# Attention tile loads and second-layer weight transfers put behind the attention matmul bursts in a planned xLSTM and two-layer MLP kernel

## The chip, the cores and the metric

The kernel runs on one core of a Trainium2 chip. The metric is the device time of one execution in microseconds (us). Engines are named as in the profile: PE is TensorE's matmul side, PEld its weight loads, DVE is VectorE, ACT is ScalarE, POOL is GpSimd, SP is SyncE, which here issues all data transfers.

## What is computed

An mLSTM attention over 4 batches, 8 heads, 768 steps and head size 40, and behind it two dense MLP layers on the 3072 x 320 result:

```python
C = f_stab * C + i_stab * (v k^T)
n = f_stab * n + i_stab * k
y = sigmoid(o) * (C q) / max(|n q|, 1)

h = x @ w_in          # 320 -> 2048
x = max(0.01 * h, h) @ w_out
h = x @ w_in2
x = (h * cos(h)) @ w_out2
```

Gates are stabilised by a running maximum, `m`. The weights come as float64 and are used in two float32r halves.

## The kernel before

**Work.** The sequence is cut into 12 chunks of 64 steps; a chunk of two batches is one attention tile, 24 in all (`ORDER`, line 90). A tile gives 128 rows of the MLP's input. The first layer takes these rows in eight blocks of 4, 2, 3, 3, 3, 3, 3 and 3 tiles (`BLOCKS1`), the second in eight blocks of 3. A block runs over 16 slices of the 2048 hidden columns; a slice is eight input matmuls (`m_in`, line 871), a nonlinearity on ScalarE and VectorE with a split into a high and a low half, and three output matmuls per tile (`m_out`, line 939). While a block of the first layer runs, the attention tiles of the next block are made between its slices. Layer 2 has no attention.

**An attention tile.** `a_qk` loads q and k (two loads), `a_fb` the forget factors (two loads of broadcast rows), `a_kvo` k, v and the output gate. VectorE scans the factors (`a_scan`), scales v and k (`a_vext`, `a_kt`) and weighs the scores (`a_weigh`). From tile 6 on (`FUSED`) one task of small TensorE matmuls, `a_fused` (line 666, matmuls at line 681), holds what tile c still needs of TensorE (its output and its state update) and what tile c+1 needs first (its scores and its part from the old state). In the text this is the burst of tile c; its key in the plan is `("out", c)`. Behind it come `a_ys`, `a_norm`, `a_scale` and `a_gate` (line 784, writes tile x), and x is transposed (`x_turn`, line 523) for the block.

**Weights.** Each of the 32 slices of weights is loaded as raw 64-bit words (`w_load`, line 429) and decoded by ScalarE and VectorE (`w_bits`, `w_tail`, `w_sign`, `w_round`, `w_mask`). Those of layer 1 stay in SBUF. Those of layer 2 are decoded during layer 1, stored to memory (`w_store`, line 458) and loaded again (`w_reload`) when the last block of layer 1 lets go of its slices.

**Order.** `Schedule.run` (line 107) is a planner that runs when the kernel is built. Every task has a due time `prio`, an engine with an estimated duration, `deps` (tasks that must be done in the plan), rings it takes and frees (buffers), and at times an earliest start `after`. The planner simulates engines and one DMA pipe; at each step it takes the task that can start first, and among those within 0.02 us the one with the smallest `prio`. The result is a fixed order of instructions for each engine. On the chip an instruction waits only for the data and buffers that it touches, in that order; `deps` makes no semaphore by itself. SP too issues its transfers in this order, each waiting for its buffer.

Due times of attention tasks are a tile's target `t_need` less an offset: `OFF` and `OFF0` for early tiles, `OFF1` (line 80) for tiles 6 and later. Loads, scan and some others of a fused tile count from the target of the tile before (`e1`, line 796). For the weights of layer 2 the due times of the decoding are spread evenly from `t0` to `t1` (line 498, from `W2`). Rings: q and k (`raw`) 3 buffers, `kvo` 3, `fb` 2, raw weights 3, decoded weights `wf` 4, output tiles `o` 2. `fb` of tile c is let go by the burst of tile c, `raw` of tile c by the burst of c-1, `kvo` of tile c by its burst and its gate.

Of the kernel before, what the change touches and what calls it, by code (L numbers as in the profile page):

```python
# [21 lines left out]
B, H, S, D = 4, 8, 768, 40  # L22
P = 128
# [4 lines left out]
NC = B * NCI  # L28
DP = 48
HD = H // 2  # L30
E1 = D + 1
# [7 lines left out]
KV = OO + DM  # L39
O_C, O_S = HD * E1, 512 - HD * E1  # L40
FUSED = 6
# [4 lines left out]
WC = 3 * P + DM  # L46
# [22 lines left out]
PACED = [10.0, 100.0]  # L69
TURNS = {0: -2.528, 1: -18.819}  # L70
GATES_TOO = -11.804
W2 = {0: -14.132, 1: -44.746}
OFF = {
    "fb": 135.274, "kvo": -62.905, "qk": 98.808, "vext": 3.999, "scan": -61.587, "kt": 2.172, "s": 10.837, "weigh": 64.711, "out": 101.947,
    "sig": 32.187, "ym": 41.146, "ys": -6.596, "norm": 54.306, "scale": -49.255, "gate": -53.487, "state": 112.532, "decay": 89.366, "tr": 0.153,
# [2 lines left out]
}  # L78

OFF1 = {  # L80
    "fb": 34.118, "kvo": -42.575, "qk": 35.553, "vext": 6.558, "scan": 27.336, "kt": -15.482, "s": -73.643, "weigh": -9.209, "out": 14.51, "sig": -4.322, "ym": 69.268, "ys": 98.299, "norm": -20.307, "scale": 155.47, "gate": 171.825, "state": 137.837, "decay": -16.852, "tr": 139.583,
}


# [101 lines left out]
def mlstm_moe(ctx, tc, qk, kvo, gates, w1, w2, out):  # L186
# [24 lines left out]
    col = cp.tile([P, NS, 3, 2 * H], F32, name="col")  # L211
# [7 lines left out]
    sch = Schedule()  # L219
# [13 lines left out]
    def dvp(n):  # L233
        return ("DVE", 0.065 + n * 0.00105)
# [10 lines left out]
    def dma(cols, parts=P, pace=False):  # L245
        return dict(size=cols * 4 * parts / 255e3, pace=pace)

    SP = ("SP", 0.45)
# [173 lines left out]
    wt, wraw, wf, wsg = {}, {}, {}, {}  # L422
# [46 lines left out]
        w = wt[l, i]  # L469
        on[eng].tensor_tensor(w[:, 1, :], wf.pop((l, i)), w[:, 0, :].bitcast(F32), ALU.subtract)  # L470

    def plan_decode(l, i, p, after=0.0):
        k = (l, i)
        wide = dma(2 * WC if double[l] else WC, pace=True)
        if not double[l]:
            sch.add(("wload", k), p - 6, SP, w_load, l, i, take=[("wf", k, 1)], after=after, **wide)
            return ("wload", k)
        sch.add(("wload", k), p - OFF["w_load"], SP, w_load, l, i, take=[("raw64", k, 1)], after=after,
                **wide)
        sch.add(("bits", k), p, ("DVE", 0.435, "port"), w_bits, l, i, deps=[("wload", k)], take=[("wf", k, 1)])  # L480
        sch.add(("tail", k), p, act(WC), w_tail, l, i, deps=[("wload", k)])
        sch.add(("sign", k), p + 0.1, act(WC), w_sign, l, i, deps=[("wload", k)], take=[("sg", k, 1)])
        sch.add(("round", k), p + OFF["w_round"], [dve(WC)] + pool(WC, l), w_round, l, i, deps=[("bits", k), ("tail", k), ("sign", k)],
                free=[("raw64", k)])
        sch.add(("mask", k), p + OFF["w_mask"], dve(WC), w_mask, l, i, deps=[("round", k), ("sign", k)], free=[("sg", k)])
        return ("mask", k)
# [6 lines left out]
    def plan_weights():  # L493
        for i in range(NF):
            p = t_slot[0, 0, i] - DEC_LEAD
            plan_split(0, i, p + OFF["w_hi"], plan_decode(0, i, p))
        n = len(BLOCKS1) - 1
        t0, t1 = t_slot[0, 2, 0] + W2[0], t_slot[0, n, 0] - W2[1]
        for i in range(NF):
            p = t0 + (t1 - t0) * i / NF  # L500
            dep = []
            if double[1]:
                d = plan_decode(1, i, p, after=p - 8)
                sch.add(("wstore", i), p + 3, SP, w_store, i, deps=[d], free=[("wf", (1, i))], **dma(WC))
                dep = [("wstore", i)]
            p = t_slot[0, n, i] + 6
            sch.add(("reload", i), p - 8, SP, w_reload, i, deps=dep, take=[("wf", (2, i), 1)], after=p - 9, **dma(WC))
            k = (1, i)
            sch.add(("whi", k), p, [act(WC), dve(WC, True)], w_hi, 1, i, deps=[("reload", i)], take=[("w", k, 1)])
            sch.add(("w", k), p + 0.1, [dve(WC)] + pool(WC), w_lo, 1, i, deps=[("whi", k)], free=[("wf", (2, i))])  # L510
# [275 lines left out]
    heads, heads_ps = ("ACT", 1.78), ("ACT", 1.45)  # L786

    def plan_attention(n, c, j, m):
# [5 lines left out]
        g, late = s // NG, n > 1  # L794
        fused, sc = c >= FUSED, ("out", c - 1) if c > FUSED else ("s", c)
        e1 = t_need[c - 1] if c > FUSED else e
        for hh in range(2):
            sch.add(("qk", c, hh), e1 - off["qk"] + 0.1 * hh, SP, a_qk, c, hh, take=[] if hh else [("raw", c, 1)],
                    deps=[("qk", c, 0)] if hh else [], **dma(10 * P, DP, pace=True))
        sch.add(("kvo", c), e1 - off["kvo"], SP, a_kvo, c, take=[("kvo", c, 2)], **dma(KV, pace=True))  # L800
        if c < SPREAD:
            sch.add(("fb", c), e - off["scan"] - 2, ("PE", 1.15), a_spread, c, deps=[("cut", 0), "ident"],
                    take=[("acc", ("fp", c), 1), ("fb", c, 1)])
        else:
            for r in range(2):
                sch.add(("fb", c, r), e1 - off["fb"] + 0.1 * r, SP, a_fb, c, r, deps=[("fb", c, 0) if r else ("sf", g)],
                        take=[] if r else [("fb", c, 1)], **dma(H * T, T))
        sch.add(("scan", c), e1 - off["scan"], ("DVE", 1.13) if c < SPREAD else ("DVE", 1.13, "port"), a_scan, c,
                deps=([("fb", c)] if c < SPREAD else [("fb", c, 0), ("fb", c, 1)]) + ["eye"],
# [2 lines left out]
        kt = []  # L812
# [9 lines left out]
            sch.add(("s", c), e - off["s"], ("PE", 0.66 + (0.45 if s else 0)), a_scores, c, deps=ready(c),  # L822
                    take=[("p", (c, a), 1 + (not own) + (not last)) for a in range(2)])
        if s:
            sch.add(("ym", c), e1 - off["ym"], ("DVE", 0.8) if fused else [dvp(H * E1), heads_ps], a_inter, c, deps=[sc, ("col", min(g, 1))], take=[("y", c, 1)],
                    free=[("p", (("s", c) if c == FUSED else c - 1, a)) for a in range(2)] if fused else [])
        sch.add(("weigh", c), e1 - off["weigh"], dvp(4 * P), a_weigh, c, deps=[sc, ("scan", c)] + kt, free=[("tr", ("s", c))] if fused else pair_)
        sch.add(("sig", c), e - off["sig"], ("ACT", 0.36), a_sig, c, deps=[("kvo", c), ("exp", 0, 0), ("exp", 0, 1)], table="sig")
# [276 lines left out]
```

## Time and profile before

| what | value |
|---|---|
| runs | 816.35, 817.06, 820.85 us; median 817.06 |
| the profiled execution's own time | 815.58 us |
| its span, first to last instruction | 813.8 us |
| PE, PEld busy | 98%, 94% |
| DVE, ACT, POOL busy | 77%, 54%, 3% |
| granted TensorE clock, mean | 0.998 of full speed |
| moved by DMA | 74.49 MB, 92 GB/s in the mean |

The profile shows one execution. Matmuls are pipelined, so a busy PE is one that always has a matmul under way, not one at its peak. Durations below are from this execution; its span is 1.8 us shorter than its time. The median of the runs is 1.5 us above it.

### The profile page before, as it was taken

To read this page: it belongs to the slowest core of one execution; us is meant where nothing else is said; L and a number is where in the kernel's file an instruction comes from. 1 tells how busy PE (TensorE), PEld (TensorE's weight loads), DVE (VectorE), ACT (ScalarE), POOL (GpSimd) and SP (SyncE) were. 2 spreads that over 40 slices of the span, in tenths; PEclk is the share of its full clock that TensorE was granted. 3 is DMA by queue.
4 is the path that set the end of the run, shared out by engine and by line. 5 is a ranking of instruction groups with operands and counts; after the bars stand their busy time and mean duration, and the time that the engine had idled before them with its cause. 6 is when DMAs were issued, how large, how long until landed. Compare 5 with 4: busy or idle time off the path is not lost.

```text
span 813.8 us, 19227 instructions
## 1 busy us (share of the span) xinstructions
PE 799.1 (98%) x7807; PEld 768.0 (94%) x7818; DVE 623.4 (77%) x1324; ACT 438.9 (54%) x961; POOL 21.6 (3%) x33
## 2 busy tenths in 40 slices
PE   8989999999999999999999999999999999999998
PEld 4669899999999999999999999999999999999998
DVE  8889968558475577655657788889797988888885
ACT  4569644434444444443445656556565656565664
POOL 1000001011000000000000000000000000000000
PEclk9999999999999999999999999999999999999999
DMA  5667535336253435413325201000000000010000
GB/s 160 213 210 232 163 102 194 103 121 177 87 168 102 164 95 176 144 60 125 124 96 185 97 9 33 17 18 29 21 25 25 25 25 26 15 35 10 17 10 24
DMA packets 29944, 74.49 MB, mean 92 GB/s; under 512 B 4384, under 2 KB 13728, under 8 KB 29856
## 3 DMA queue, kind: packets, MB, share of 16 engines
q1 hardware_dynamic: 29856, 73.27, 28.1%
q8 instruction: 61, 1.00, 0.5%
q14 instruction: 27, 0.22, 0.1%
HBM read 59.54 MB, written 13.71 MB: 90 GB/s over the span
## 4 chain that ended last, share of the span: by engine, by line
PE 86%; DVE 7%; DMA 3%; ACT 2%; issue 1%; ACTq 0%; SPq 0%; DVEq 0%
PE acc L939 37%; PE ph L871 34%; PE pair L871 6%; PE pair L681 2%; PE tr L523 2%; DMA kvo<-kvo 2%; PE busy L274 2%; DMA raw<-w 2%; PE sc L681 1%; DVE gl L919 1%; DVE fb L688 1%; ACT ph L880 1%; DVE wf L455 1%; DVE y L756 0%; DVE x L784 0%
## 5 line engine op out<-in xcount | busy, mean ns | idle before, releaser
L939 PE MATMUL acc<-w,gh 128*128 128x320 f32 x1568 | 347.4, 309 | 0.0
L871 PE MATMUL ph<-xt,w 128*128 128x384 f32 (+2 forms) x1760 | 344.7, 338 | 2.1 <-DVE gl L919 1.9
L871 PEld LDWEIGHTS ph<-xt,w 128*128 128x128 f32 x1760 | 298.0, 189 | 7.6 <-DVE gl L919 2.6
L939 PEld LDWEIGHTS acc<-w,gh 128*128 128x128 f32 x1568 | 265.6, 188 | 1.8
L939 PE MATMUL acc<-w,gl 128*128 128x320 f32 (+1 forms) x784 | 239.0, 308 | 0.4 <-DVE gl L919 0.4
L939 PEld LDWEIGHTS acc<-w,gl 128*128 128x128 f32 x784 | 146.3, 188 | 0.6 <-DVE gl L919 0.6
L919 DVE TENSOR_TENSOR gl<-ph,gh 128x384 fp32r<-128x384 f32 (+2 forms) x124 | 68.7, 554 | 89.9 <-ACT ph L880 86.4
L879 ACT ACTIVATE gh<-ph 128x384 fp32r<-128x384 f32 (+2 forms) x124 | 60.8, 490 | 124.3 <-PE ph L871 105.7
L901 ACT ACTIVATE r<-r,hpi 128x384 f32<-128x384 f32 x128 | 78.9, 616 | 69.9 <-DVE r L897 69.8
L224 ACT CAST gh<-g 128x384 fp32r<-128x384 f32 x128 | 65.6, 513 | 39.9 <-PE acc L939 17.2
L919 DVE TENSOR_TENSOR gl<-g,gh 128x384 fp32r<-128x384 f32 x127 | 70.4, 559 | 9.2 <-ACT gh L224 9.2
L907 DVE TENSOR_TENSOR g<-ph,r 128x384 f32<-128x384 f32 x96 | 52.6, 555 | 13.9 <-ACT r L901 12.7
L880 ACT ACTIVATE ph<-ph 128x384 f32<-128x384 f32 (+2 forms) x124 | 60.6, 489 | 0.0
L871 PE MATMUL pair<-xt,w 128*128 128x384 f32 x288 | 55.9, 336 | 0.0
L896 DVE SCALAR_TENSOR_TENSOR r<-t,ph 128x384 f32<-128x384 f32 x96 | 53.2, 554 | 3.3
L887 ACT ACTIVATE t<-ph 128x384 f32<-128x384 f32 x96 | 46.7, 487 | 13.6 <-PE ph L871 8.0
L893 DVE TENSOR_SCALAR t<-t 128x384 f32<-128x384 f32 x128 | 45.6, 356 | 7.0 <-ACT t L887 4.1
L897 DVE TENSOR_SCALAR r<-r 128x384 f32<-128x384 f32 x128 | 46.1, 360 | 4.4
L871 PEld LDWEIGHTS pair<-xt,w 128*128 128x128 f32 x288 | 49.4, 188 | 0.0
L224 ACT CAST xt<-tr 128x256 fp32r<-128x256 f32 x104 | 27.6, 316 | 25.2 <-PE tr L523 23.1
L470 DVE TENSOR_TENSOR w<-wf,w 128x704 fp32r<-128x704 f32 x32 | 28.3, 888 | 2.3 <-ACT w L224 1.9
L443 ACT ACTIVATE raw<-raw 128x704 f32<-128x704 uint32 x32 | 27.3, 853 | 3.6 <-DMA raw<-w 3.4
(120 smaller groups left out, 707.0 us busy)
## 6 DMA issues: line engine op xcount, KB each, us to landing
raw<-w SPq DMA_DIRECT2D x32, 704.0 KB, 4.5
kvo<-kvo SPq DMA_DIRECT2D x24, 484.0 KB, 3.6
raw<-qk SPq DMA_DIRECT2D x48, 192.0 KB, 3.7
w2d<-wf SPq DMA_DIRECT2D x16, 352.0 KB, 3.0
wf<-w2d SPq DMA_DIRECT2D x16, 352.0 KB, 3.1
fb<-sfd SPq DMA_DIRECT2D x40, 128.0 KB, 3.4
x2d<-o SPq DMA_DIRECT2D x24, 160.0 KB, 1.8
x<-x2d SPq DMA_DIRECT2D x24, 160.0 KB, 2.2
```

Source lines behind the costliest of these rows:

```text
L224: nc.scalar.copy(dst, src)
L871: nc.tensor.matmul(ph[:, :N], w[:, a:a + P], x[:, b, :N], start=k == 0, stop=k == 7)
L879: nc.scalar.activation(t["gh"][:, :N], h, AF.Prelu, alpha=0.01)
L880: nc.scalar.activation(h, h, AF.Prelu, alpha=0.01)
L887: nc.scalar.activation(t["a"][:, :N], t["h"][:, :N], AF.Copy, scale=1.0 / TWO_PI, bias=0.25)
L893: nc.vector.tensor_scalar(a, a, MAGIC, -MAGIC, ALU.add, ALU.add)
L896: nc.vector.scalar_tensor_tensor(r, a, -TWO_PI, t["h"][:, :N], ALU.mult, ALU.add)
L897: nc.vector.tensor_scalar(r, r, -4.712388, 1.5707959, ALU.max, ALU.min)
L901: nc.scalar.activation(r, r, AF.Sin, bias=hpi)
L907: nc.vector.tensor_tensor(t["g"][:, :N], t["h"][:, :N], t["r"][:, :N], ALU.mult)
L919: on[eng].tensor_tensor(t["gl"][:, :N], t["g"][:, :N], t["gh"][:, :N].bitcast(F32), ALU.subtract)
L939: nc.tensor.matmul(po, a[:, s], w[:, b, e], start=i == 0 and k == 0 and j < 3, stop=i == NF - 1 and k == 2, skip_group_check=True,)
```

## The change

Four things are edited. (1) The offsets `OFF1` of tiles 6 and later, and `W2`, get other values. (2) The loads of a tile c of 8 or more (q and k, k-v-o, forget factors) get a planner dependency, `gap`, on the burst of tile c-2. (3) The raw load of the i-th weight slice of layer 2 loses its earliest start and depends in the plan on the burst of tile 8+i (at most 22), with a due time just behind that burst's; its store depends on the burst of tile 9+i (at most 23) in the same way. (4) The planner's duration of `ym` for fused tiles goes from 0.80 to 0.92 us. No operation is added, removed or reshaped.

```diff
--- before.py
+++ after.py
@@ -69,7 +69,7 @@
 PACED = [10.0, 100.0]
 TURNS = {0: -2.528, 1: -18.819}
 GATES_TOO = -11.804
-W2 = {0: -14.132, 1: -44.746}
+W2 = {0: -5.09, 1: -46.716}
 OFF = {
     "fb": 135.274, "kvo": -62.905, "qk": 98.808, "vext": 3.999, "scan": -61.587, "kt": 2.172, "s": 10.837, "weigh": 64.711, "out": 101.947,
     "sig": 32.187, "ym": 41.146, "ys": -6.596, "norm": 54.306, "scale": -49.255, "gate": -53.487, "state": 112.532, "decay": 89.366, "tr": 0.153,
@@ -78,7 +78,7 @@
 }
 
 OFF1 = {
-    "fb": 34.118, "kvo": -42.575, "qk": 35.553, "vext": 6.558, "scan": 27.336, "kt": -15.482, "s": -73.643, "weigh": -9.209, "out": 14.51, "sig": -4.322, "ym": 69.268, "ys": 98.299, "norm": -20.307, "scale": 155.47, "gate": 171.825, "state": 137.837, "decay": -16.852, "tr": 139.583,
+    "fb": 141.244, "kvo": -44.251, "qk": 83.644, "vext": 2.87, "scan": -51.184, "kt": 39.885, "s": -10.115, "weigh": 55.797, "out": 25.103, "sig": 106.513, "ym": -18.386, "ys": 85.126, "norm": 53.109, "scale": 23.084, "gate": 57.877, "state": 152.634, "decay": -90.507, "tr": 175.728,
 }
 
 
@@ -469,13 +469,13 @@
         w = wt[l, i]
         on[eng].tensor_tensor(w[:, 1, :], wf.pop((l, i)), w[:, 0, :].bitcast(F32), ALU.subtract)
 
-    def plan_decode(l, i, p, after=0.0):
+    def plan_decode(l, i, p, after=0.0, gap=()):
         k = (l, i)
         wide = dma(2 * WC if double[l] else WC, pace=True)
         if not double[l]:
             sch.add(("wload", k), p - 6, SP, w_load, l, i, take=[("wf", k, 1)], after=after, **wide)
             return ("wload", k)
-        sch.add(("wload", k), p - OFF["w_load"], SP, w_load, l, i, take=[("raw64", k, 1)], after=after,
+        sch.add(("wload", k), gap[1] if gap else p - OFF["w_load"], SP, w_load, l, i, deps=gap[:1], take=[("raw64", k, 1)], after=after,
                 **wide)
         sch.add(("bits", k), p, ("DVE", 0.435, "port"), w_bits, l, i, deps=[("wload", k)], take=[("wf", k, 1)])
         sch.add(("tail", k), p, act(WC), w_tail, l, i, deps=[("wload", k)])
@@ -500,8 +500,10 @@
             p = t0 + (t1 - t0) * i / NF
             dep = []
             if double[1]:
-                d = plan_decode(1, i, p, after=p - 8)
-                sch.add(("wstore", i), p + 3, SP, w_store, i, deps=[d], free=[("wf", (1, i))], **dma(WC))
+                c = [min(FUSED + 2 + i + j, NC - 1) for j in range(2)]
+                q = [t_need[x] - OFF1["out"] for x in c]
+                d = plan_decode(1, i, p, gap=[("out", min(c[0], NC - 2)), q[0] + 0.2])
+                sch.add(("wstore", i), q[1] + 0.1, SP, w_store, i, deps=[d, ("out", c[1])], free=[("wf", (1, i))], **dma(WC))
                 dep = [("wstore", i)]
             p = t_slot[0, n, i] + 6
             sch.add(("reload", i), p - 8, SP, w_reload, i, deps=dep, take=[("wf", (2, i), 1)], after=p - 9, **dma(WC))
@@ -794,16 +796,17 @@
         g, late = s // NG, n > 1
         fused, sc = c >= FUSED, ("out", c - 1) if c > FUSED else ("s", c)
         e1 = t_need[c - 1] if c > FUSED else e
+        gap = [("out", c - 2)] if c - 2 >= FUSED else []
         for hh in range(2):
             sch.add(("qk", c, hh), e1 - off["qk"] + 0.1 * hh, SP, a_qk, c, hh, take=[] if hh else [("raw", c, 1)],
-                    deps=[("qk", c, 0)] if hh else [], **dma(10 * P, DP, pace=True))
-        sch.add(("kvo", c), e1 - off["kvo"], SP, a_kvo, c, take=[("kvo", c, 2)], **dma(KV, pace=True))
+                    deps=[("qk", c, 0)] if hh else gap, **dma(10 * P, DP, pace=True))
+        sch.add(("kvo", c), e1 - off["kvo"], SP, a_kvo, c, deps=gap, take=[("kvo", c, 2)], **dma(KV, pace=True))
         if c < SPREAD:
             sch.add(("fb", c), e - off["scan"] - 2, ("PE", 1.15), a_spread, c, deps=[("cut", 0), "ident"],
                     take=[("acc", ("fp", c), 1), ("fb", c, 1)])
         else:
             for r in range(2):
-                sch.add(("fb", c, r), e1 - off["fb"] + 0.1 * r, SP, a_fb, c, r, deps=[("fb", c, 0) if r else ("sf", g)],
+                sch.add(("fb", c, r), e1 - off["fb"] + 0.1 * r, SP, a_fb, c, r, deps=[("fb", c, 0)] if r else [("sf", g)] + gap,
                         take=[] if r else [("fb", c, 1)], **dma(H * T, T))
         sch.add(("scan", c), e1 - off["scan"], ("DVE", 1.13) if c < SPREAD else ("DVE", 1.13, "port"), a_scan, c,
                 deps=([("fb", c)] if c < SPREAD else [("fb", c, 0), ("fb", c, 1)]) + ["eye"],
@@ -822,7 +825,7 @@
             sch.add(("s", c), e - off["s"], ("PE", 0.66 + (0.45 if s else 0)), a_scores, c, deps=ready(c),
                     take=[("p", (c, a), 1 + (not own) + (not last)) for a in range(2)])
         if s:
-            sch.add(("ym", c), e1 - off["ym"], ("DVE", 0.8) if fused else [dvp(H * E1), heads_ps], a_inter, c, deps=[sc, ("col", min(g, 1))], take=[("y", c, 1)],
+            sch.add(("ym", c), e1 - off["ym"], ("DVE", 0.92) if fused else [dvp(H * E1), heads_ps], a_inter, c, deps=[sc, ("col", min(g, 1))], take=[("y", c, 1)],
                     free=[("p", (("s", c) if c == FUSED else c - 1, a)) for a in range(2)] if fused else [])
         sch.add(("weigh", c), e1 - off["weigh"], dvp(4 * P), a_weigh, c, deps=[sc, ("scan", c)] + kt, free=[("tr", ("s", c))] if fused else pair_)
         sch.add(("sig", c), e - off["sig"], ("ACT", 0.36), a_sig, c, deps=[("kvo", c), ("exp", 0, 0), ("exp", 0, 1)], table="sig")
```

## Rows read from the trace of the kernel before

**Rows 1.** The page: busy time (share, instructions) of TensorE; queue 8 (packets, MB, share).

```profile
PE 799.1 (98%) x7807; PEld 768.0 (94%) x7818; DVE 623.4 (77%) x1324; ACT 438.9 (54%) x961; POOL 21.6 (3%) x33
...
q8 instruction: 61, 1.00, 0.5%
```

**Rows 2.** Waits of TensorE: us in total, times, longest us.

```profile
PE pair L681 <- issue: 1.8, 1, 1.8
PE tr L523 <- DVE x L784: 1.7, 6, 0.5
```

**Rows 3.** Timeline of TensorE in the burst of tile 8: start us, us, instruction.

```profile
144.67 0.25 PE L681 MATMUL pair<-state,raw 40*64 40x41 f32 x1 [1.79 <-issue]
```

**Rows 4.** Windows: length; busy (instructions) of five engines; PEclk, DMA share, GB/s.

```profile
131.13:133.05 1.92, 1.92 (x130) 1.87 (x129) 0.90 (x2) 0.54 (x2) 0.00 (x0) 1.00 0.08 19
141.06:145.04 3.98, 2.19 (x129) 1.99 (x128) 1.28 (x3) 0.54 (x2) 0.00 (x0) 1.00 0.63 244
145.04:148.51 3.47, 3.47 (x17) 3.47 (x15) 3.18 (x8) 1.30 (x4) 0.73 (x1) 0.51 0.34 99
148.51:150.34 1.83, 1.83 (x15) 1.83 (x15) 1.03 (x4) 1.59 (x4) 0.00 (x0) 1.00 0.00 0
```

**Rows 5.** Window and DMA queue 8 from 500 to 600 us, in layer 2.

```profile
500.00:600.00 100.00, 100.00 (x635) 99.91 (x634) 86.47 (x197) 62.56 (x132) 0.00 (x0) 1.00 0.08 26
...
q8 instruction: 5, 0.08, 0.3%
```

**Rows 6.** DMA queues: all from 133.9 to 142.1 us; queue 8 from 142.1 to 143.1.

```profile
q1 hardware_dynamic: 555, 1.82, 67.6%
...
q8 instruction: 1, 0.02, 5.9%
```

**Rows 7.** Timeline of SP ahead of the burst of tile 8.

```profile
137.82 0.35 SPq L599 DMA_DIRECT2D kvo<-kvo  x1
138.21 0.43 SPq L429 DMA_DIRECT2D raw<-w  x1
```

**Rows 8.** The page's DMA issues: count, KB each, median us to landing.

```profile
raw<-w SPq DMA_DIRECT2D x32, 704.0 KB, 4.5
kvo<-kvo SPq DMA_DIRECT2D x24, 484.0 KB, 3.6
raw<-qk SPq DMA_DIRECT2D x48, 192.0 KB, 3.7
w2d<-wf SPq DMA_DIRECT2D x16, 352.0 KB, 3.0
...
fb<-sfd SPq DMA_DIRECT2D x40, 128.0 KB, 3.4
```

**Rows 9.** Windows of 5 us that end with bursts, and one full stretch.

```profile
128.00:133.00 5.00, 5.00 (x153) 4.80 (x151) 3.32 (x7) 2.30 (x8) 0.00 (x0) 1.00 0.46 143
...
164.30:169.30 5.00, 5.00 (x150) 4.81 (x148) 1.05 (x3) 1.90 (x6) 0.00 (x0) 1.00 0.24 94
...
330.30:335.30 5.00, 5.00 (x149) 4.75 (x147) 2.32 (x4) 2.57 (x6) 0.00 (x0) 1.00 0.04 15
341.30:346.30 5.00, 5.00 (x149) 4.75 (x147) 2.98 (x7) 2.28 (x6) 0.00 (x0) 1.00 0.81 265
...
140.09:141.05 0.96, 0.96 (x8) 0.77 (x6) 0.93 (x3) 0.66 (x2) 0.69 (x1) 1.00 1.05 403
```

**Rows 10.** Waits of SP's queue: us in total, times, longest us.

```profile
SPq L579 <- PE pair L681: 72.0, 16, 8.7
...
SPq L599 <- DVE x L784: 39.0, 16, 5.2
```

**Rows 11.** Groups of VectorE instructions, 100 to 404 us: busy, mean ns, idle before.

```profile
L604 DVE TENSOR_TENSOR_SCAN fb<-fb,eye 128x512 f32<-128x512 f32 x18 | 22.0, 1221 | 0.8 <-DMA fb<-sfd 0.6
...
L623 DVE TENSOR_TENSOR kvo<-kvo,fb 128x320 f32<-128x320 f32 x10 | 4.9, 486 | 0.1
```

**Rows 12.** Window from 100 to 404 us, columns as in rows 4.

```profile
100.00:404.00 304.00, 299.76 (x4035) 290.46 (x4034) 198.79 (x412) 130.15 (x332) 17.19 (x22) 0.99 0.40 129
```

## The prediction

> **What bounds the kernel now.** Read the page's head first: TensorE is busy for 799.1 us, 98% of the span, so a change off TensorE is worth what it takes out of TensorE's own row [rows 1]. Next the waits of TensorE, longest first: in the stretch that the change touches two count. One is 1.8 us in one piece before an attention matmul, with "issue" as its end (nothing that the profile shows was waited for); the other are six waits, 1.7 us together, of the transposes for the gated tile [rows 2].
>
> The 1.8 us deserve the timeline. The burst of a tile (64 fp32 products, each two matmuls and two weight loads in the trace) is normally short: the one at 131.13 us gives way to the next large matmul 1.92 us later. The next burst, at 141.06 us, runs dry before its last matmuls and goes on at 144.67 us after 1.79 us of idle time [rows 3], so that 3.98 us pass [rows 4]. Then look behind it: the same eight matmuls of line 871 and six of line 939 take 3.47 us at a granted clock of 0.51 (1.2 GHz instead of 2.4), and 1.83 us at 1.00 right afterwards [rows 4]. Before it fell, the engine had stood idle for that 1.79 us. So **one stall costs 2.06 + 1.64 = 3.70 us**.
>
> What ran out? Not operands: no semaphore ended it. What does arrive by DMA is code. The page has 61 packets of kind "instruction" on queue 8 [rows 1]; in a stretch of layer 2 five come in 100 us, in which TensorE starts 635 matmuls and 634 weight loads [rows 5], so one packet serves about 254 instructions. A burst uses 130 + 129 in under 2 us [rows 4], as much as a whole packet. In the 8.2 us up to 142.1 us queue 8 moved nothing, while the data queue was busy at 67.6%; the packet came in the next microsecond [rows 6]. What filled it was a kvo load let go by tile 7's gate (line 784) at 137.82 us and a 704 KB raw weight load right after it [rows 7], which together take long to land [rows 8]. I read the stall as a late code packet behind those loads. Of the 17 bursts from 131 us on, in windows of 5 us that end with them, five had the transfers busy at 0.46 to 0.81 and twelve at 0.24 or less; one of the five stalled, none of the twelve [rows 9]. A loaded queue is needed, but so is the place of the packet's border in the burst.
>
> **The change, part by part.** No instruction is added or removed; due times and two kinds of planner dependency move.
>
> The gap. `deps` is known to the planner alone: on the chip an SP entry waits for buffers. But SP works in order, and fb of tile c has two buffers, so its first load waits for the burst of c-2; SP does this 16 times already, 72.0 us in all [rows 10]. With fb's due time moved from 34 to 141 us ahead, it is planned first behind the burst, and qk (84 ahead), the weight load, and kvo (44 behind) stand after it. The wait thus holds on the chip for tiles from 8 on. Queued behind it on SP are also the x2d stores that free the output buffers, and for them the evacuations and TensorE's accumulators. The number of fb waits is unchanged, so I cost this at nothing. With that cover gone the bound is SP's longest fb wait, 8.7 us, if at a block's end a store stood behind it with both output buffers full.
>
> At the burst of tile 8 the kvo load of tile 10 and the weight load are no longer in flight: both now come behind it. The 3.70 us go. What is late next: the code packet that a burst asks for now meets fb and qk behind the burst, but there TensorE uses about 13 instructions per us [rows 5], not 130.
>
> Earlier bursts. Bursts are due 25.1 instead of 14.5 us before their tile's due time. The gate chain behind them may end earlier against its transposes: bounds are a gain of all 1.7 us [rows 2] and a loss of as much, if the new order drifts the other way. I take a gain of half of it, 0.9 us, since the due time is earlier; not more, because the planner still puts a transpose as soon as it thinks it ready.
>
> Later loads. Before, kvo of tile c+3 was let go by the gate of c [rows 10]; now kvo of c+2 comes last behind the burst of c. Up to it SP moves 2x128 + 2x192 + 352 + 704 + 484 = 2180 KB, 2.23 MB [rows 8]. At 403 GB/s, the rate of a full stretch [rows 9], that is 5.5 us. SP needs about 0.4 us to issue the first [rows 7], and kvo's 3.6 us to landing leave, less its 484 KB at that rate (1.2), 2.4 us that do not shrink: 8.3 us. VectorE then scales k in 0.49 us, its scan (1.22 us) having been done on fb meanwhile [rows 11]: 8.8 us. The shortest distances from a burst's end to the next burst are 8.0 us (133.05 to 141.06 us [rows 4], where no weights come yet and the same sum gives 6.2) and 9.1 us (windows that end at 335.3 and 346.3 us [rows 9], less a burst). At all others it is 10 us or more. So it fits, by 0.3 us at the tightest. Cost 0; if VectorE is late, up to a microsecond per burst (rival below).
>
> Weights of layer 2. The first raw load moves behind tile 8's burst, the last two behind tile 22's. Due times of the decoding start 9.0 us later and end 2.0 us later. Same VectorE and ScalarE work, with VectorE busy 199 of the 304 us from 100 to 404 [rows 12]: nothing. The dearer `ym` (0.92 for 0.80) changes the plan's clock alone, no operation.
>
> Sum against the profiled execution (815.58 us, span 813.8): 815.58 - 3.70 - 0.9 = 811.0. The three runs have a median of 817.06, 1.5 above it, and one lies at 820.85, which is 3.8 above the median, the price of one more stall. Taking the difference from the median: **812.4 us**.
>
> The Trainium skill speaks against the main term. "Runtime: NRT & Kernel Launch", section on instruction fetch mechanics, says the sequencer fetches the next 16 KiB block of 256 instructions while it executes, at a cost that is mostly hidden. This trace agrees on the block (61 packets, 1.00 MB) and not on the cover: by the page the stall term would be 0 and the sum 816.2.
>
> **Rivals.** *The stall moves or was never the loads'.* For it: four bursts with loaded queues did not stall [rows 9], and every due time of tiles 6 on is new, so the packet borders fall elsewhere in the bursts; tiles 6 and 7 are not gated. Against: behind the gate no burst should find the queue loaded. If one stall like this remains, 3.70 is given back: 817.06 - 0.9, near 816 to 817. In "DMA: Bandwidth & Descriptors", on queues and rings, the Trainium skill says each DMA engine turns in rounds between its queues, packet by packet; by that rule a code packet would not wait out a bulk load, and the stall would stay. The quiet queue 8 up to 142.1 us [rows 6] leans against it, without deciding.
>
> *The tiles come late (slower).* With that slack gone, the PE sequencer, in order, waits for kt of tile c+1 at each burst and the large matmuls behind it wait too. It decides where load to kt takes longer than the distance of bursts. For it: 0.3 us is little, and transposes already wait for VectorE six times [rows 2]. Against: ten us and more at the other distances, and the planner itself counts these transfers before it places a burst. A scan that isn't hidden (1.22 us [rows 11]) less the 0.3 us is 0.9 us per burst; the time passes 821.1 from (821.1 - 813.4) / 15 = 0.5 us per gated burst on. Between the two, 0.7 us: 817.06 - 3.7 + 15 x 0.7 = 823.9 us.
>
> *Nothing happens.* Were fb not first on SP, qk and kvo would start early as before: 817.
>
> **Numbers.** Forecast (stall gone, no new wait) 0.53, its own range 810 to 814; the stall moves 0.15, was never the loads' 0.10, nothing happens 0.04; late tiles 0.18. About 0.5% can be told from no change, 4.1 us: faster is below 813.0, slower above 821.1. The forecast puts 0.47 below 813.0 and 0.06 in the same band; the next three, 0.29, are all "same" and late tiles all slower. The lower end, 809.0, is the forecast with both waits of [rows 2] gone wholly (0.8 more) and 2.6 us of a second stall; the upper end, 818.5, takes in the first rival and leaves out late tiles.
>
> **What would show it.** Right: no "issue" wait at line 681 among PE's waits; all bursts from 131 us 1.9 us long; granted clock 1.00 from 100 to 404 us, where 0.99 stood [rows 12]; DMA share in the windows that end with the bursts near 0; fb, qk, weights, kvo in this order on SP behind each burst. Wrong: an idle piece of 1 to 2 us in some other burst, or many waits at line 681 for a scaled k or a weighed score.

## The result, and the profile after

The changed kernel takes 808.32 us (median of 4 runs, 807.84 to 809.38), the kernel before 817.24 in the same comparison: ratio 0.9884 [0.9853, 0.9916], so faster by my 0.5%. I had 812.4, with 809.0 as the lower end. Against the kernel before as it ran in the batches below (815.6 to 816.5) it is 7.3 to 8.2 us less instead of 8.9. The profiled execution after takes 808.76 us, its span is 807.0.

The page after, its line of busy time and its row of queue 8 (answers to [rows 1]); then the longest waits of TensorE (us in total, times, longest us; [rows 2]):

```profile
PE 796.3 (99%) x7803; PEld 766.4 (95%) x7814; DVE 610.7 (76%) x1305; ACT 439.7 (54%) x967; POOL 42.2 (5%) x53
...
q8 instruction: 61, 1.00, 0.5%
```

```profile
PE ph L874 <- DVE gl L922: 2.2, 3, 1.5
PE busy L274 <- DVE gm L298: 1.0, 1, 1.0
PE acc L942 <- DVE gl L922: 0.6, 1, 0.6
```

The 1.8 us with "issue" as their end are gone, and so are all waits of the transposes for the gated tile. (The four instructions fewer are warm-up fillers, which the planner places by its own clock.) Windows over the bursts of tiles 7 and 8, and from 100 to 404 us (columns as in [rows 4]):

```profile
132.26:134.18 1.92, 1.92 (x130) 1.87 (x129) 0.42 (x1) 0.72 (x3) 0.00 (x0) 1.00 0.04 9
143.83:145.75 1.92, 1.92 (x130) 1.87 (x129) 0.42 (x1) 0.72 (x3) 0.00 (x0) 1.00 0.00 0
...
100.00:404.00 304.00, 302.98 (x4075) 295.87 (x4074) 191.35 (x400) 135.05 (x341) 37.80 (x42) 1.00 0.44 135
```

The burst of tile 8 takes 1.92 us instead of 3.98 [rows 4], the granted clock is 1.00 where 0.99 stood [rows 12], and TensorE is busy 3.2 us more of the 304. SP behind the burst of 175.24 us goes in the order that I had read off the due times:

```profile
176.79 0.45 SPq L581 DMA_DIRECT2D fb<-sfd  x1
177.30 0.65 SPq L574 DMA_DIRECT2D raw<-qk  x1
...
179.58 0.45 SPq L429 DMA_DIRECT2D raw<-w  x1
180.13 0.46 SPq L601 DMA_DIRECT2D kvo<-kvo  x1
```

One sign that I had named did not come: the transfers are not near 0 ahead of the bursts. Of the 16 bursts of tiles 7 to 22, four have them busy at 0.31 or more in the 5 us before, tile 22's at 0.87 and tile 20's at 0.63, and none stalls:

```profile
333.81:338.81 5.00, 5.00 (x32) 4.75 (x31) 3.92 (x7) 3.38 (x7) 0.00 (x0) 1.00 0.63 191
```

Where the time went, by the first input matmul of blocks 1, 2 and 7 in the timelines, first before, then after:

```profile
115.75 0.32 PE L871 MATMUL ph<-xt,w 128*128 128x256 f32 x1
156.14 0.34 PE L871 MATMUL ph<-xt,w 128*128 128x384 f32 x1
411.85 0.34 PE L871 MATMUL ph<-xt,w 128*128 128x384 f32 x1
```

```profile
115.52 0.32 PE L874 MATMUL ph<-xt,w 128*128 128x256 f32 x1
152.52 0.34 PE L874 MATMUL ph<-xt,w 128*128 128x384 f32 x1
405.22 0.34 PE L874 MATMUL ph<-xt,w 128*128 128x384 f32 x1
```

Behind block 7's start both take the same 402 us. So of the 6.8 us between the two spans 0.2 lie up to block 1, 3.4 in block 1 (the stall's block), 3.0 in blocks 2 to 6. The other two of the nine lie between profiled execution and median (below). The 0.2 is too small a figure for the start: the execution profiled after ran a stretch of its warm-up at half clock, the one before did not. Window over it, then block 1's start in a run with the new due times and no such stretch (e3 below), 1.8 us ahead of before:

```profile
10.70:14.10 3.40, 3.40 (x9) 0.93 (x8) 3.03 (x9) 1.61 (x2) 0.00 (x0) 0.50 0.46 107
```

```profile
113.97 0.32 PE L871 MATMUL ph<-xt,w 128*128 128x256 f32 x1
```

### The profile page after: what moved, and what is told of

It is laid out like the page before. It is cut to its first block, busy times and chain, and to the rows that moved or that the text cites. A ratio compares the mean times of both kernels' runs of the same rounds, so it can differ in the third digit from the quotient of the medians.

```text
span 807.0 us, 19223 instructions
## 1 busy us (share of the span) xinstructions
PE 796.3 (99%) x7803; PEld 766.4 (95%) x7814; DVE 610.7 (76%) x1305; ACT 439.7 (54%) x967; POOL 42.2 (5%) x53
## 4 chain that ended last, share of the span: by engine, by line
PE 93%; DVE 3%; DMA 2%; issue 1%; ACT 0%; SPq 0%; DVEq 0%; ACTq 0%
PE acc L942 41%; PE ph L874 37%; PE pair L874 6%; PE pair L683 3%; PE tr L525 2%; PE busy L274 2%; DMA kvo<-kvo 1%; PE sc L683 1%; DMA fb<-sfd 1%; DVE fb L606 1%; DVE gl L922 0%; DVE gm L313 0%; PE pair L645 0%; PE acc L711 0%; DVE w L470 0%
```

## Experiments

Medians are of ten executions unless said; "before" in one batch with them was 815.6 to 816.5. The second number is the ratio to that, with its interval; an interval that takes in 1 cannot be told from no change.

**e1, the kernel before once more.** Edit: a blank line at the end.

> The kernel before, unchanged, to see what one execution of it differs from another in. Theory A (stalls behind loads come in some executions more often than once): its spans differ in steps of 3 to 4 us, and executions above 816 us show a granted clock lower than the 0.998 of the profiled one, or a second idle piece in a burst. Theory B (the 1.5 us by which the median lies above the profiled execution are spread evenly): same clock in all, same single stall at the burst of tile 8. Both: time 816 to 818, ratio 1.00.

816.30 us, 1.0003 [0.998, 1.0025]. The mean granted clock of the ten executions runs from 0.989 to 1.000, so not the same in all (theory A). In the profiled one the stall of tile 8's burst is there again (1.5 us idle), one of 0.7 at tile 16's burst as well, and near 50 us something that the first profile does not have. The start of block 0, timelines of TensorE, first the kernel before as first profiled, then e1:

```profile
41.68 0.49 PE L523 MATMUL tr<-ident,x 128*128 128x128 f32 x3
...
43.30 2.58 PE L274 MATMUL busy<-hpi 128*128 128x512 bf16 x11
45.52 2.20 PE L871 MATMUL ph<-xt,w 128*128 128x512 f32 x8
49.63 2.12 PE L871 MATMUL ph<-xt,w 128*128 128x512 f32 x8 [1.90 <-DVE gl L919]
```

```profile
41.07 0.49 PE L523 MATMUL tr<-ident,x 128*128 128x128 f32 x3
44.92 2.19 PE L871 MATMUL ph<-xt,w 128*128 128x512 f32 x8
49.02 3.31 PE L871 MATMUL ph<-xt,w 128*128 128x512 f32 x8 [1.90 <-DVE gl L919]
```

After the same 1.90 us of idle time the same eight matmuls take 2.12 us in one execution and 3.31 in the other, in a window (49.0 to 52.5 us) whose granted clock is 0.59. So one program differs by a microsecond in block 0 and by 0.9 in a second stall; this is why its runs spread and its median lies above the execution that I reckoned from.

**Which edit? e2, e3, e12.** e2 is the changed kernel with the old due times, so it has the new dependencies and the new `ym`; e3 is the kernel before with the new due times (`OFF1` and `W2`) alone; e12 the kernel before with `OFF1` alone. (Long lines are cut at `...`, here and below.)

```diff
-W2 = {0: -5.09, 1: -46.716}                                  # e2
+W2 = {0: -14.132, 1: -44.746}
-    "fb": 141.244, "kvo": -44.251, ...
+    "fb": 34.118, "kvo": -42.575, ...
-W2 = {0: -14.132, 1: -44.746}                                # e3
+W2 = {0: -5.09, 1: -46.716}
-    "fb": 34.118, "kvo": -42.575, ...                        # e3, e12
+    "fb": 141.244, "kvo": -44.251, ...
```

> The new planner dependencies (tile loads behind the burst of c-2, weight loads and stores behind bursts) with the offsets and W2 of the kernel before. If the gain comes from loads kept out of the bursts, no idle piece at a burst and 812 to 814 us, with the waits of the transposes still there; if the gain needs the new due times, the stall stays somewhere, 815 to 818.

> The new offsets and W2 without the new dependencies. If the dependencies are what removes the stall, at least one burst stalls (3.7 us each) and 812 to 817 us; if the new due times alone do it, under 810 and no stall.

> The offsets OFF1 alone, with the W2 and the planner dependencies of before. If W2 matters little: 807 to 809 us, as with both; if the decoding's later start is what clears the burst of tile 8, a stall stays and 811 to 813.

e2: 816.32, 0.9996 [0.9978, 1.0013]. e3: 807.87 (4 runs), 0.9885 [0.9845, 0.9926]. e12: 808.57 (8 runs), 0.9917 [0.988, 0.9953]. So **the offsets of the due times bring the whole gain, and the dependencies of the title none**: without them 807.9, with them 808.3. Whether `W2` adds anything cannot be told: e3 and e12 lie 0.7 us apart, and their intervals overlap. In e2 no burst stalls, but other waits come, TensorE's list:

```profile
PE ph L874 <- DVE gl L922: 2.7, 3, 1.9
PE acc L942 <- DVE gl L922: 1.7, 4, 0.7
...
PE tr L525 <- DVE x L786: 0.8, 3, 0.5
```

In e3 the queues are loaded ahead of bursts and none stalls by more than 0.25 us. Two of its windows of 5 us that end with a burst, DMA share 0.74 and 0.78, against which [rows 9] stand:

```profile
161.71:166.71 5.00, 5.00 (x34) 4.78 (x32) 3.85 (x8) 2.19 (x6) 0.00 (x0) 1.00 0.74 253
...
224.13:229.13 5.00, 5.00 (x34) 4.81 (x33) 3.40 (x7) 1.78 (x6) 0.26 (x1) 1.00 0.78 275
```

**Is it the loads? e4, e6, e9.** The kernel before with one, two and three loads behind tile 8's burst in the plan.

```diff
-a_kvo, c, take=[("kvo", c, 2)]
+a_kvo, c, deps=[("out", 8)] if c in (10, 11) else [], take=[("kvo", c, 2)]   # e6: c == 10
-w_load, l, i, take=[("raw64", k, 1)], after=after,
+w_load, l, i, take=[("raw64", k, 1)], after=after, deps=[("out", 8)] if k == (1, 1) else [],  # e4, e6, e9
```

> The kernel before with one planner dependency more: the raw load of weight slice 1 of layer 2 behind the burst of tile 8. Theory (a late code packet behind loads): the idle piece at the burst of tile 8 goes or shrinks below 1 us, 813 to 814 us (minus 3.7). Rival (the stall has nothing to do with loads): it stays at 1.8 us, with 817.

> The kernel before with both loads that ran into the burst of tile 8 (raw weights of slice 1, kvo of tile 10) behind it in the plan. Theory (loads delay the code packet): no idle piece at that burst, 812 to 814 us. Rival: still over 1 us of idle there, as with the weight load alone, 815 to 816.

> The kernel before with the raw weight load of slice 1 and the kvo loads of tiles 10 and 11 behind the burst of tile 8 (in the run with two loads the planner had put the kvo load of tile 11 in the freed place). Theory (loads delay the code packet): no idle piece over 0.5 us at that burst and no slow clock at 145 us, 3 to 3.7 us less in block 1; 812 to 813.5 us. Rival: 0.9 us of idle stays, 814 to 816.

e4: 815.55, 0.9987 [0.9962, 1.0011], idle 1.2 us. e6: 814.0, 0.9981 [0.9954, 1.0007], idle 0.9; the planner put another kvo load into the free place. None of the three times can be told from before; the profiles decide. In e9 (814.74, 0.9986 [0.9955, 1.0016]) nothing is left in flight; windows of 1 us up to the burst at 141.51, and TensorE's wait:

```profile
139.00:140.00 1.00, 1.00 (x10) 1.00 (x9) 1.00 (x2) 0.53 (x3) 0.00 (x0) 1.00 0.00 0
140.00:141.00 1.00, 1.00 (x10) 1.00 (x10) 0.95 (x4) 0.20 (x1) 0.54 (x1) 1.00 0.00 0
141.00:142.00 1.00, 1.00 (x36) 0.81 (x39) 1.00 (x3) 0.46 (x2) 0.20 (x1) 1.00 0.00 0
142.00:143.00 1.00, 1.00 (x94) 1.00 (x85) 0.35 (x2) 0.17 (x1) 0.00 (x0) 1.00 0.16 56
143.00:144.00 1.00, 0.33 (x22) 0.21 (x14) 0.00 (x0) 0.00 (x0) 0.00 (x0) 1.00 0.80 307
```

```profile
PE pair L681 <- issue: 1.5, 1, 1.5
```

Moved bytes 0 for three microseconds, and the stall stays. **My reading of the stall falls here**: the code packet is late, it came at 142.43 us, 0.9 us into the burst, but with no load ahead of it.

**What makes the packet late? e5, e13, e15, e16.** TensorE's queue has a row that I had passed over. Semaphore waits of the queue (PEldq) at line 681 in the kernel before, from 138 to 142 us (ns least, median, most; first and last start):

```profile
L681 PEldq EVENT_SEMAPHORE  x1: 1775/1775/1775, 138.6 to 138.6; - x1
```

The burst's scores share a PSUM buffer with the transposes (tag `tr`, one buffer). The queue, which runs ahead of the matmuls, stands at the burst until VectorE has emptied the transposes of tile 7 (line 536, 140.06 + 0.28 us), that is until 140.4. In all eleven bursts of tile 8 (tile 7 in e5) that stalled by 0.9 us or more, the packet started 0.9 to 2.3 us after the end of this wait: 1.75 in the kernel before, loads in flight, and 1.62 in e9, none in flight. e5 moves the border of the packets by 126 instructions (21 warm-up matmuls in four pieces each). e13 takes the wait away: tile 7's transposes go behind the burst by hand. e15 makes such a wait at tile 8's burst in e12, where there is none.

```diff
+            for j in range(4):                                  # e5, e16
+                nc.tensor.matmul(gt["busy"][:, j * P:(j + 1) * P], i.to_broadcast([P, P]), i.to_broadcast([P, P]), ...)
+        t = order.pop(at_task('x_turn', 0, 2, 7))               # e13; x_hi and x_lo likewise
+        order.insert(at_task('m_out', 0, 1, 2, 10), t)
+        t = order.pop(at_task('x_lo', 0, 2, 7))                 # e15
+        order.insert(at_task('m_lo', 0, 1, 2, 10), t)
+            for _ in range(2):                                  # e15, in x_lo of tile 7
+                nc.vector.tensor_tensor(xt[:, 2, s], tr[:, 0, :], ...)
```

> The kernel before, with 21 of the warm-up matmuls at the start cut into four pieces each: 126 TensorE instructions more, the same columns, the same plan and the same loads. Theory (a code packet of 254 instructions late behind loads): every packet border falls about half a packet earlier in the work, so the idle piece at the burst of tile 8 goes though its loads are the same, and another loaded burst may get one; 812 to 814 us if none does. Rival (the idle piece belongs to that place or to its loads alone): it stays at tile 8, 816.

> The kernel before, with the transposes of the gated tile 7 and their two splits moved by hand from ahead of the burst of tile 8 to three slices behind it; every load stays where it was, and the packet's border falls 6 matmuls and 6 weight loads (0.02 of a packet) later in the burst. Theory now (the sequencer is held): scores and transposes share one PSUM buffer, so TensorE's sequencer stands at the burst until VectorE has emptied the transposes' buffer (1.77 us, until 140.4 us in the trace of before), asks for the next code packet only then, and the packet comes 0.9 to 1.1 us into a burst that uses 260 instructions in 1.9. Without the wait the packet comes ahead of the burst or in its first tenths: no stall, burst 1.9 us, granted clock 1.0 behind it, 3 us off: 812 to 813.5. Rival, the border alone: the stall of 1.5 to 2 us stays wherever a border falls like this, 816. Rival, the loads: they are still in flight, so the stall stays as well.

> The kernel with the new offsets alone (808.6, no stall, the border in the same place: 0.74 of a packet at the start of tile 8's burst), with VectorE's split of the transposed tile 7 put behind the scaling of k and its first part done three times over (the same values), so that it ends at about 140, half a microsecond before the burst, instead of 138.6. Nothing moves on TensorE. Theory (sequencer held): the stall of before appears, 1.2 to 2 us idle in the burst of tile 8 and a stretch at half clock behind it, 3 us more: 811 to 812.5. Rival (the border alone, or the loads, which are unchanged at a DMA share of 0.75): no stall, 808.6 and at most the 0.6 us by which VectorE is later.

> The new due times without the new dependencies (807.9), with 17 of the warm-up matmuls late in the start in four pieces each: 102 instructions more, 0.40 of a packet, so that the border falls at 0.72 of a packet at the start of tile 16's burst, where the sequencer is held for 2.35 us until 0.56 us before the burst. Theory: a stall of 1.2 to 2 us in that burst, 2 to 3.5 us more (810 to 811.5) besides what the longer warm-up costs. Rival (loads, or chance): no stall there, 808 plus the warm-up's cost.

e5: 819.22, 1.0051 [1.0025, 1.0077], slower. But the stall has moved, from tile 8's burst to tile 7's, both of which have a wait of the queue ahead (1.77 and 2.37 us):

```profile
138.72:142.44 3.72, 2.19 (x130) 2.00 (x129) 0.90 (x2) 0.64 (x2) 0.00 (x0) 1.00 0.13 47
151.88:153.80 1.92, 1.92 (x130) 1.87 (x129) 1.28 (x3) 0.54 (x2) 0.00 (x0) 1.00 0.88 352
```

The burst with the transfers at 0.88 is clean, the one at 0.13 stalls. A second idle piece, 1.1 us, stands right behind tile 14's burst, where the queue had waited 1.58 us. e13: 814.54, 0.9987 [0.997, 1.0004], 1.0 to 2.5 us above what I had expected, and not to be told from before; but the stall is gone. The code packet came at 139.31 us, 3.1 us ahead of the burst. The kvo and weight loads of before were let go only behind it, at 139.74 and 140.13 us, so this run does not show a packet that has to pass loads. Waits of the queue, the burst's window, and what TensorE waits for instead:

```profile
L681 PEldq EVENT_SEMAPHORE  x2: 51/51/51, 140.0 to 140.3; - x2
```

```profile
142.40:144.30 1.90, 1.90 (x129) 1.86 (x128) 1.19 (x3) 0.57 (x2) 0.95 (x1) 1.00 1.03 426
```

```profile
PE tr L523 <- DVE xt L536: 1.0, 1, 1.0
```

Block 1 is 2.5 us shorter than before (37.92 for 40.39), the 3.5 of the stall less this 1.0.

e15: 809.59 (8 runs), 0.9928 [0.9909, 0.9948], no stall in tile 8's burst, a miss. The wait is there, 1.64 us long and over 0.7 us ahead of the burst, but the packet came during it. e16: 810.47 (4 runs), 0.9929 [0.9901, 0.9957], no stall in tile 16's burst, a miss in the same way: a wait of 2.10 us, and the packet within it. So the wait alone is not enough; the kernel before has one of 1.81 us at tile 7's burst, too, and no stall there.

Nor is a wait always needed. e16 has an idle piece behind tile 7's burst (it begins at 132.40 us), where e3, with the same order and 102 instructions fewer ahead, has none. Waits of the queue, the 4 us up to the burst with the transfers at 0.93, and the weight loads behind it:

```profile
L686 PEldq EVENT_SEMAPHORE  x2: 51/51/51, 129.9 to 132.6; - x2
```

```profile
128.40:132.40 4.00, 4.00 (x32) 3.81 (x31) 3.26 (x8) 1.48 (x6) 0.00 (x0) 1.00 0.93 287
```

```profile
134.31 0.19 PEld L876 LDWEIGHTS ph<-xt,w 128*128 128x128 f32 x1
135.39 0.19 PEld L876 LDWEIGHTS ph<-xt,w 128*128 128x128 f32 x1 [0.89 <-issue]
```

The packet came 0.37 us into that burst. The stall of tile 16's burst in e1 is alike: in the first profile of before the same burst has the same transfers ahead (0.96 to 1.07) and nearly the same wait (0.57 us, e1 0.61, over 2.3 us ahead), but its packet came 1.5 us before the burst, in e1 0.1 us into it. And e12 has 1.1 us of idle behind tile 19's burst, with a wait of 1.82 us and the transfers at 0.86.

What all of these runs allow: a burst runs dry when the code packet that it needs comes late, and whether it needs one hangs on the packet's border. A wait of the queue can make it late with no load in flight (e9), and at tile 8 taking the wait away took the stall away (e13). Loads may make it late without such a wait (e16); no run was made to test that. Where the border lies to a dozen instructions cannot be counted from the trace, and the two misses leave this half argued.

**The transposes: e7, e14, e10.** e7 makes the planner alone believe that a transpose is ready 0.8 us later (a task on an engine that does not exist); nothing on the chip is slower, transposes just stand later on TensorE. e14 adds e13's move, e10 the three loads of e9.

```diff
+        if l == 0 and c >= FUSED:
+            sch.add(("lag", c), p, ("LAG", 0.8), lambda eng: None, deps=[dep])
+        sch.add(("tr", l, c), p, ..., deps=[dep, ...] + ([("lag", c)] if l == 0 and c >= FUSED else []), ...)
```

> The kernel before, with 0.8 us added in the plan alone between a gated tile (6 and later) and its transposes. Theory (transposes planned too early cost 3 us in blocks 2 to 6, by TensorE's start times): the waits of the transposes for line 784 go, 2 to 3 us less, 813. Rival (the gain of blocks 2 to 6 comes from elsewhere): less than 1 us, 815 to 816.

> The same hand move on top of the lag of 0.8 us that the planner puts between a gate and its transposes (which alone gave 811.0, with the stall still there). Theory: both terms together, 816.2 - 4.4 - 3.3, near 808.5, are the change's whole gain, from none of its loads and none of its due times. Rival, the gain of the due times is something else besides: the time stays at 811, or the two do not add up and it is above 810.

> The run before with the planned lag of 0.8 us before the transposes as well. If stall and transposes are the whole gain of the change, 808 to 810 us, as the changed kernel; if the new due times bring something else of over 1 us, 810 to 812.

e7: 811.03, 0.9946 [0.9923, 0.9969], by the ratio 4.4 us from this alone (2.5 to 6.3), its stall still there in the profile (2.0 us). Its blocks 2 to 6 take 252.3 us, the kernel before 255.7, the change 252.7. e14: 811.56 (5 runs), 0.9947 [0.9927, 0.9966]: 3.0 less than e13, but not the 808.5 of two full terms; its rival came, something else is in the gain. e10: 812.83, 0.9962 [0.9932, 0.9992], the stall there (1.4 us). How much the transposes cost is seen better on the weight-load side. Idle time of that engine ahead of line 523 in the kernel before, by what ended it (us, times):

```profile
  issue: 3.6, 8
  DVE x L784: 2.2, 7
```

Of these 5.8 us, 5.3 lie between 100 and 404 us (14 pieces). After the change neither line is there.

**e8 and e11**, six fillers into the idle piece at 47 us, and the earlier due time of the bursts alone (`"out": 25.103`):

> The kernel before with six more filler matmuls behind the first slice of block 0, where TensorE stands idle for 1.9 us at 47 us. Theory (this idle piece drops the clock to half for 3.4 us in most executions, about 1 to 1.7 us each time, but not in the profiled one): granted clock 1.00 at 50 us in every execution, median 1 to 1.5 us lower, near 814.5. Rival (no effect on the median): 815.5 to 816.5, and clock drops there still.

> The kernel before with one number changed, the offset of the bursts' due time, 14.51 to 25.103. If an earlier due burst is what frees the transposes, their waits go and 2 to 4 us with them (812 to 814); if not, the waits stay near 1.7 us in the list and 815 to 816.

Both are misses. e8: 816.44, 1.0008 [0.9984, 1.0032]: the idle piece is 0.6 us and in the profiled execution the clock stays up there, but the planner ordered the rest anew, with eight waits of the transposes (3.0 us). e11: 818.10, 1.0025 [0.9997, 1.0054], stall and transposes' waits (1.5 us) still there, and blocks 2 to 6 take 258.1 us, 2.3 more than before. The bursts' due time alone does not do it; no other was tried alone.

**The start: e17, e18.** In the new order the first input matmuls come ahead of filler. After the change:

```profile
42.67 0.49 PE L525 MATMUL tr<-ident,x 128*128 128x128 f32 x3
...
45.21 2.19 PE L874 MATMUL ph<-xt,w 128*128 128x512 f32 x8
47.25 0.61 PE L274 MATMUL busy<-hpi 128*128 128x512 bf16 x2
49.31 2.12 PE L874 MATMUL ph<-xt,w 128*128 128x512 f32 x8 [1.45 <-DVE gl L922]
```

From the transposes to the second group it is 6.64 us, 7.95 before. e17 puts TensorE's and ScalarE's order of that by hand into the kernel before (of its three moves, TensorE's is shown), e18 adds it to e14.

```diff
+        t = order.pop(at_task("m_in", 0, 0, 4, 0))
+        order.insert(next(i for i, u in enumerate(order) if u[3].__name__ == "g_busy" and u[0] > 41.4), t)
```

> The kernel before, with only the end of its warm-up in the order that the new offsets give, by hand: the first eight input matmuls of block 0 ahead of the last six of the eleven warm-up matmuls (43.3 to 45.5 us in the trace of before), the last part of tile 3's split ahead of a weight slice's tail and sign on ScalarE, and the first nonlinearity ahead of the next such pair. Theory: this order is the third term of the gain. From tile 3's transposes to the first slice's output matmuls the profile of before takes 9.9 us and that of after 8.6, and the idle 1.9 us at 47 us, after which some executions run at half clock, are partly filled: 1.3 to 2.2 us less, 814 to 815, with the stall at tile 8's burst and the transposes' waits unchanged. Rival (the start is noise between executions): 816, no difference.

> All three hand edits on the kernel before: the start's order, tile 7's transposes behind the burst, the lag of 0.8 us ahead of the transposes; no due time, no load and no dependency of the change. Theory: 811.6 (two of them) less 1.3 to 2.2: 809.4 to 810.3, within 2 us of the change's 808.3. Rival: the start adds nothing, 811.6, and the due times have a further part of 3 us that none of the three holds.

e17: 818.02 (12 runs), 1.0026 [1.0003, 1.005]; e18: 811.9 (6 runs), 0.9946 [0.9928, 0.9964]. A miss: no gain, e17 is slower if anything. ScalarE and VectorE of e17 say why:

```profile
46.21 0.59 ACT L880 ACTIVATE ph<-ph 128x512 f32<-128x512 f32 x1
```

```profile
46.47 0.88 DVE L470 TENSOR_TENSOR w<-wf,w 128x704 fp32r<-128x704 f32 x1
47.58 0.89 DVE L451 CUSTOM_DVE_ANT_0 wf<-raw,wf 128x1408 uint16<-128x1408 uint16 x1 [0.22 <-ACT raw L443]
48.39 0.68 DVE L919 TENSOR_TENSOR gl<-ph,gh 128x512 fp32r<-128x512 f32 x1
```

The slice was ready for its split at 46.8; VectorE, whose order I had left, decoded weights until 48.4. That the new order of VectorE is what saves this microsecond or two was not tried alone. e18's rival came: 811.9 against the change's 808.3, 3.6 us that none of the three hand edits holds. Where they lie is read against e3, which like e18's profile has no stretch at half clock up to its last 2 us: e18 is 3.4 us longer, 2.5 of it up to block 1 (116.48 against 113.97), 0.4 in block 1, 0.5 in blocks 2 to 6. So what is left is mostly the start.

## Why the prediction was wrong, step by step

- **The stall goes: right in size, half right in cause.** It was priced at 3.70, and block 1 is 3.39 shorter. The late code packet stands; "behind those loads" fell with e9: no load, and a stall. "A loaded queue is needed" fell with it. The rival "never the loads'" (0.10) had that, but its time (816 to 817) assumed that the stall would then stay; the new order did away with the queue's wait at the same time. After the change no burst from 131 us on has a wait of its queue above 0.1 us. That the forecast size came out is luck in part: the gate on the loads was to bring it, and e3 has it without the gate.
- **"Earlier bursts", 0.9: the step that failed.** I took half of the 1.7 us in TensorE's list [rows 2] and called that sum the bound. It was none. Ends of matmuls are modelled and overlap the next start (in the timeline above the eleven fillers end at 43.30 + 2.58 = 45.88, the next group starts at 45.52), so a gap between groups hides in busy time; the weight-load side shows 5.8 us in 15 pieces. Measured: 3.0 us in the pair of profiles, 3.0 (medians of e13 and e14) to 4.4 (e7, by its ratio). The mechanism was wrong as well: bursts that are due earlier, alone, left the waits (e11); transposes planned later against their gates took them away (e7).
- **The start: not in the sum.** I took the new due times of tiles 6 and later to act on the bursts alone. But the order at the end of the warm-up changed too: 1.3 us less from transposes to the second group than in the first profile of before, 2.5 less to that group's end where the clock fell (e1), and 1.8 less up to block 1 where it did not (e3). Why is argued: the loads of tile 6 stand among the weight loads of the warm-up. The hand order of e17 did not bring it.
- **The baseline.** A profiled execution of before without the clock's fall near 50 us was the base, and the median carries it in part; after the change the idle piece is 1.45 instead of 1.90 us and its profile shows no fall. The nine us of the medians are thus 6.8 of the profiles and some two of executions that the old order disturbs more often. The granted clocks on record bear that out: of 130 executions of the kernel before, 20 reach 0.999, and their median is 814.25 us against 816.1 for all; of 28 with the new due times (the change, e3, e12, e15, e16), 20 do. And 817.06, the median of three runs that I started from, was itself 0.5 to 1.5 us above the later batches; from those the same sum gives 811.0 to 811.9.
- **Costs at nothing: right, as far as the runs can tell.** Dependencies (e2; e3 against the change) and SP's order; `W2` and the weights within the noise of e12 against e3.
- **Late tiles: did not come.** The distances from a burst's end to the next grew instead: 9.7 us from tile 7's to tile 8's and 11.3 to 16.3 at the others up to 338.81, where I had held 8.0 and 9.1 against a sum of 8.8. I had taken the old spacing over into a plan in which every due time was new.

In "Runtime: NRT & Kernel Launch", on instruction fetch mechanics, the Trainium skill calls the fetch mostly hidden; the trace agrees for sixteen bursts of seventeen, and where the packet came late it shows 0.7 to 2.0 us in the open. In "DMA: Bandwidth & Descriptors", on queues and rings, the Trainium skill has the engines turn between queues packet by packet; e15 agrees as far as it goes: the code packet of 139.58 us moved while data took 97% of the engines' time (139 to 140 us), and took 0.99 us of engine time (6.2% of 16 engines) against 0.97 in e13 (139.31 us, nothing else moving). How long a packet had waited before it started no run shows, and e16 and e1 leave room for that. For the stall of tile 8's burst my reading against that rule was wrong: it stayed without loads (e9).

## What to carry to other kernels

When an engine runs dry with "issue" as the end, look at its own queue first: what was the sequencer waiting for just ahead, and is a long run of short instructions behind it? Before a stall is put down to traffic, take the traffic away; a coincidence of five loaded windows and one stall looked like a cause. In a planned kernel a due time moves everything that shares an engine or a pipe with it, so price the new order, not the edited lines, and take the weight-load side's idle rows beside the matmul side's. Before two profiles are subtracted, see where each of them ran at half clock: one such stretch hid 1.5 us of the gain at the start.

## What the runs showed of the hardware

- One program, two executions: after 1.90 us of idle TensorE eight matmuls took 2.12 us in one and 3.31 in the other (granted clock 0.59 over the window).
- Splitting 21 warm-up matmuls into four pieces each (126 instructions, no more columns) left the kernel 0.5% slower (e5). Idle pieces that end with "issue" moved with it: tile 8's burst lost its own, tile 7's has 1.5 us, and 1.1 us stand behind tile 14's.
- With nothing moved by DMA, a queue of TensorE held for 1.77 us was followed by a code packet 0.9 us into a burst and 1.5 us of idle (e9). With no such wait and the transfers at 0.93, one came 0.4 us into a burst and 0.9 us of idle followed (e16).
